# All quarter sums of the part products on VectorE, GpSimd held meanwhile and its state chain one block later, squares on ScalarE, and a new order for the last block and the last products

## The chip, the core and the metric

The kernel runs on one core of one Trainium2 chip. The core has a matrix engine (TensorE, PE in the profile), three engines for elementwise work (VectorE or DVE, ScalarE or ACT, GpSimd or POOL) and SyncE (SP), which here only issues DMAs. Each engine works through its own queue in program order and waits on semaphores for the others. The metric is the device time of one execution in microseconds, the median of the runs shown.

## The reference

Two layers follow each other. The first is a retention layer with 8 batches, 8 heads, 576 positions and 64 columns a head; its result, 4608 rows of 512, is the input x of a feed-forward layer with 2048 hidden columns.

```python
gamma = 1.0 - 2.0 ** (-5.0 - np.arange(H, dtype=np.float32))
Dmat = np.where(rel >= 0, gamma[:, None, None] ** rel[None, :, :], 0.0)
ret = scores * Dmat[None, :, :, :]          # scores = q k^T / sqrt(64)
attn = np.matmul(ret, v)
...
h = x @ w_in
s = np.sin(alpha * h)
g = h + s * s / (alpha + 1e-09)
out = g @ w_out
```

All inputs and the output are float32; the kernel works in float16 with float32 accumulation.

## The kernel before, in words

The 4608 rows are handled as 9 blocks of 512: block b is the first 512 positions of batch b, and block 8 (NBLK is 9, its input is the tile xS) holds the last 64 positions of all batches. The order of instructions on every engine is written out by hand; there is no scheduler. Up to block 2 it is a flat list, from block 3 on the loop `for n in range(3, NBLK)`.

One block of the feed-forward layer is 16 units, one for each 128 hidden columns. A unit u is: `project` (4 matmuls of 512 columns into a bank of PSUM, tile hps, line 550), `sine` on ScalarE (tile s, 558), `square` (tile ss, ScalarE at 567, VectorE or GpSimd at 569) and `product` on VectorE (574), which writes g transposed into gT and frees the bank. Three banks, h0 to h2, are taken in turn, so a projection can start when the product three units before it (two, where attention has taken a bank) is done.

The second matmul, g times w_out, runs one block later, between the projections of the next block. Up to block 2 it is done plainly (`gemm2`, 593, and `finish`). From block 3 on gT and w_out are cut into quarters, and seven products of quarters, M1 to M7, take the place of eight (Strassen's scheme in Winograd's form). `row_sum` (640) makes the sums of gT's quarters S1 to S4, each in two halves p = 0 and 1 (hidden columns 0 to 1023 and 1024 to 2047, that is units 0 to 7 and 8 to 15); S3 is written over a quarter of gT, S1 and S4 need S2. `weight_sum` (630) makes T1 to T4 of w_out once; T1 is written over a quarter of w_out, which the plain products of block 2 still read in block 3. `part_product` (659) runs one product of 16 matmuls of 256 columns; the list `slots` tells after which pair of units each comes. `after_product` (689 to 703) adds up the results: M1 is copied by ScalarE to the tile low (689); M2 is added in M1's bank and copied by ScalarE to an output tile osb (701); M6 gives the tile mid (691), M7 in the same bank gives a new low (693); M4, M5 and M3 are added to these into osb (703). `store` (674, and 670 for block 8) sends osb out, from SyncE's queue but for the very last pieces; in block 8 each output tile takes 4 DMAs.

The attention of batch n+1 runs within block n: `scores` at two units, `masked` on VectorE (385), and at unit `turns` the value products in two halves, with a mark by GpSimd between them (`told`, an empty instruction on GpSimd that waits for the first half and that the second half waits for), the states' part, and `keep` on ScalarE, which writes xT for the next block. At the same unit `outer` makes the products of k and v of batch n+2, ScalarE evicts them (`evict_bank`), and GpSimd turns them into running states: `chain`, which is `to_state` (347) and `more` (354, 355) for four chunks. GpSimd also casts k, v and q of batch n+2 (195 and 122), one each from unit c0 on, and the ends of the batches (179). The loads that bring them go through SyncE's queue into four raw buffers; a load of q takes the place that a cast of k or v in the same block frees. `crossed` are transposing DMAs of the casts, also on SyncE's queue.

What is done around unit u is collected in two lists: `at_unit(u, ...)` runs after the unit's sine, `behind(u, ...)` after its product. In blocks 4 to 8 the squares of the units in ON_V are on VectorE and the others on ScalarE. Block 3 (`plain`) has rules of its own, since the plain products of block 2 run in it.

Before the change, VectorE makes S3 and S2, and GpSimd makes both halves of S1 and S4 behind unit 1 of the next block. After the last block the seven products of block 8 follow in the order M4, M1, M6, M2, M7, M5, M3, with sums on VectorE and GpSimd in between.

## Time and profile before

| | before |
|---|---|
| runs, us | 317.64, 318.65, 322.0 |
| median, us | 318.65 |
| the profiled execution's own time, us | 316.81 |
| its span, first to last instruction, us | 315.1 |
| mean granted TensorE clock in it | 0.993 |

The profile is of one execution. Its page gives busy times by engine, the share of busy time in 40 slices, the DMA queues, the chain of work that ended last and the costliest groups of instructions. A row of the timeline has start, duration, engine, line and operation, out<-in, the shape, and in brackets the idle time of the engine before it and who ended that. A row of a group has the busy time in us, the mean ns of one, and the idle time before them with its releasers. A row of the table by stretches has, for each engine, the busy us and the count of instructions, then the granted TensorE clock, the DMA engines' busy share and GB/s. A row of the waits has the total in us, how often, and the longest. PE is TensorE's matmuls, PEld its weight loads, SPq and ACTq are DMA issues. Instruction starts can overlap the end of the one before by some 0.1 us, since an engine's pipeline takes the next one early.

### The profile page before, as it was taken

What the parts mean: (1) busy time and instruction counts of PE and PEld (TensorE: products, weight loads), DVE (VectorE), ACT (ScalarE), POOL (GpSimd) and SP (SyncE); (2) the same over time, 40 slices, a digit from 0 to 9 for tenths busy, and PEclk for the clock granted to TensorE, in tenths of its full rate; (3) what the DMA queues carried; (4) which work ended last, traced back from release to release, by engine and by line L of the source; (5) the groups of instructions that cost most, each with busy time, mean ns of one, the idle gap of its engine ahead of it and who ended that gap; (6) DMA issues with size and microseconds to landing.
All of it is one profiled execution on the core that took longest, in us unless ns stands there. A gap on an engine that the chain in (4) does not pass through costs nothing.

```text
span 315.1 us, 8517 instructions
## 1 busy us (share of the span) xinstructions
PE 288.3 (91%) x3480; PEld 183.6 (58%) x3480; DVE 247.5 (79%) x333; ACT 195.1 (62%) x321; POOL 188.5 (60%) x173
## 2 busy tenths in 40 slices
PE   5889999999989999997799989898999999989682
PEld 4676445555445544555366666565767676666471
DVE  2578886976269779979996999799889868987861
ACT  1669837987758967775258655856576566654300
POOL 4793688483877865697944897989225501630420
PEclk9999999999999999999799999999999999999999
DMA  8999999997899789896828878964571122102113
GB/s 225 345 215 213 262 302 312 229 249 206 185 230 180 168 181 253 147 189 131 225 61 118 185 185 223 173 144 122 120 115 37 41 45 68 33 2 67 33 35 101
DMA packets 123527, 50.09 MB, mean 159 GB/s; under 512 B 80480, under 2 KB 121440, under 8 KB 123488
## 3 DMA queue, kind: packets, MB, share of 16 engines
q1 hardware_dynamic: 119968, 45.17, 61.4%
q0 software_dynamic: 2688, 4.19, 7.3%
q8 instruction: 27, 0.44, 0.5%
q10 hardware_dynamic: 832, 0.18, 0.4%
q14 instruction: 12, 0.10, 0.1%
HBM read 36.75 MB, written 9.44 MB: 147 GB/s over the span
## 4 chain that ended last, share of the span: by engine, by line
PE 47%; DVE 25%; DMA 13%; ACT 6%; issue 3%; SPq 2%; POOL 2%; POOLq 0%; DVEq 0%; ACTq 0%
PE hps L550 24%; PE ops L659 12%; PE ops L593 7%; DVE gT L574 7%; DVE ss L569 5%; DMA raw<-in_k_dram 4%; DMA raw<-in_v_dram 4%; DVE S L640 4%; DVE gT L640 3%; DMA w_in<-in_moe_w_in_dram 3%; ACT s L558 2%; DVE ret L385 2%; ACT ss L567 2%; DMA qT<-q 1%; PE o L415 1%
## 5 line engine op out<-in xcount | busy, mean ns | idle before, releaser
L558 ACT ACTIVATE s<-hps,alpha_t 128x512 f16<-128x512 f32 x144 | 97.3, 683 | 65.5 <-PE hps L550 64.6
L550 PE MATMUL hps<-xT,w_in 128*128 128x512 f16 (+1 forms) x532 | 123.3, 374 | 5.3 <-DVE gT L574 4.8
L574 DVE SCALAR_TENSOR_TENSOR gT<-ss,inva,hps 128x512 f16<-128x512 f16 x144 | 105.8, 744 | 28.0 <-ACT ss L567 24.1
L550 PEld LDWEIGHTS <-w_in 128*128 128x128 f16 x596 | 66.8, 114 | 59.1 <-issue 10.2
L640 POOL TENSOR_TENSOR S<-gT,S 128x1024 f16<-128x1024 f16 x22 | 49.1, 2252 | 49.8 <-DVE S L640 42.0
L567 ACT ACTIVATE ss<-s 128x512 f16<-128x512 f16 x84 | 52.7, 630 | 2.3
L593 PE MATMUL ops<-w_out,gT 128*128 128x512 f16 x192 | 46.8, 380 | 0.0
L659 PEld LDWEIGHTS <-gT 128*128 128x128 f16 x384 | 36.8, 98 | 10.2 <-DVE gT L574 1.8
L569 DVE TENSOR_TENSOR ss<-s 128x512 f16<-128x512 f16 x52 | 38.1, 735 | 5.2 <-ACT s L558 5.2
L195 POOL TENSOR_TENSOR k<-raw,cn 128x1024 f16<-128x1024 f32 (+1 forms) x17 | 29.4, 1734 | 8.4 <-DMA raw<-in_k_dram 6.9
L659 PEld LDWEIGHTS <-S 128*128 128x128 f16 x288 | 28.0, 98 | 9.2 <-issue 1.6
L593 PEld LDWEIGHTS <-gT 128*128 128x128 f16 x192 | 17.9, 98 | 20.4
L195 POOL TENSOR_TENSOR q<-raw,cn 128x1024 f16<-128x1024 f32 x13 | 25.1, 1938 | 6.4 <-DMA raw<-in_q_dram 4.9
L659 PE MATMUL ops<-T,gT 128*128 128x256 f16 x192 | 23.3, 273 | 2.0 <-DVE gT L574 1.5
L659 PE MATMUL ops<-w_out,S 128*128 128x256 f16 x192 | 23.1, 273 | 1.3 <-DVE osb L703 1.3
L659 PE MATMUL ops<-w_out,gT 128*128 128x256 f16 x192 | 23.0, 273 | 0.0
L385 DVE TENSOR_TENSOR ret<-sc,mask 128x1024 f16<-128x1024 f32 x16 | 19.2, 1220 | 2.9 <-PE sc L373 2.9
L355 POOL TENSOR_TENSOR kvs<-s,kvs 128x256 f32<-128x256 f32 x21 | 17.4, 830 | 3.7 <-ACT kvs L120 1.3
L347 POOL TENSOR_TENSOR s<-kvs,cn 128x256 f16<-128x256 f32 x17 | 10.8, 635 | 11.3 <-PE o L437 7.6
L550 PE MATMUL hps<-xS,w_in 128*128 128x512 f16 x64 | 15.6, 379 | 1.5 <-DVE gT L574 1.4
L354 POOL TENSOR_TENSOR s<-kvs,cn 128x256 f32<-128x256 f32 x21 | 13.0, 620 | 6.5 <-ACT kvs L120 6.4
L373 PE MATMUL sc<-qT,kT 64*64 64x128 f16 (+1 forms) x512 | 11.4, 222 | 4.7 <-DVE ret L385 3.5
(78 smaller groups left out, 286.3 us busy)
## 6 DMA issues: line engine op xcount, KB each, us to landing
raw<-in_q_dram SPq DMA_DIRECT2D x16, 512.0 KB, 4.7
out_dram<-osb SPq DMA_DIRECT2D x64, 128.0 KB, 2.6
raw<-in_k_dram SPq DMA_DIRECT2D x8, 512.0 KB, 6.4
raw<-in_v_dram SPq DMA_DIRECT2D x8, 512.0 KB, 6.5
raw<-in_v_dram SPq DMA_DIRECT2D x32, 128.0 KB, 3.2
raw<-in_k_dram SPq DMA_DIRECT2D x32, 128.0 KB, 3.0
w_in<-in_moe_w_in_dram POOLq DMA_DIRECT2D x4, 512.0 KB, 11.6
w_out<-in_moe_w_out_dram POOLq DMA_DIRECT2D x4, 512.0 KB, 12.9
```

The costliest lines, as they stand in the source:

```text
L195: eng.tensor_tensor(dst[:, a0:a1].rearrange("p a r t d -> p t (a r) d"), t_.rearrange("p (t a) x -> p t a x", t=2)[:, :, a0:a1].rearrange( ...
L354: nc.gpsimd.tensor_tensor(s32, self.kvs[:, c - 1], g1.unsqueeze(2).to_broadcast([P, 4, D]), MULT)
L355: nc.gpsimd.tensor_tensor(self.kvs[:, c], s32, self.kvs[:, c], ADD)
L385: nc.vector.tensor_tensor(ret.rearrange("p t (z x) -> p (t z) x", z=2)[:, :, 0:n], sc.rearrange("p t (z x) -> p (t z) x", z=2)[:, :, 0:n], ...
L550: matmul(hps_of[n, fc][0][:, cols], w_in16[fc // 4][:, a, fc % 4 :: 4], xs[n][:, a, cols], start=(a == 0 and part != 1), stop=(a == KT - 1 ...
L558: nc.scalar.activation(s_t, hps, mybir.ActivationFunctionType.Sin, bias=0.0, scale=alpha_t[:, fc : fc + 1],)
L567: nc.scalar.activation(ss_t, s_t, mybir.ActivationFunctionType.Square)
L569: eng.tensor_tensor(ss_t, s_t, s_t, MULT)
L574: nc.vector.scalar_tensor_tensor(gT[n][:, fc, :], ss_t, inva[:, fc : fc + 1], hps, MULT, ADD)
L593: matmul(ops[n, c, cols.start][:, cols], gT[n][:, fk, c * P : (c + 1) * P], w_out16[:, fk, cols], start=(fk == 0), stop=(fk == FC - 1), sk ...
L640: eng.tensor_tensor(out_, x, y, op)
L659: matmul(acc[:, 256 * j : 256 * j + 256], lhs[:, x, 128 * j : 128 * j + 128], rhs[:, x], start=(tag is not None and j == 0 and p == 0 and ...
```

## The change

1. GpSimd makes no sums any more. VectorE makes all of them: S3, S2, S1 and S4 of the first half behind units 11, 13 and 15 of the block itself, those of the second half behind units 0, 1 and 2 of the next block.
2. Behind unit 2 an empty instruction on GpSimd waits for the last sum, and only then comes the state chain, which stood at unit 13 of the block before. The casts start one unit later (c0 is 5, not 4).
3. In blocks 4 and 5 only the squares of units 12, 13 and 14 are on VectorE, in blocks 6 to 8 those of 2, 6, 10, 12, 13 and 14. The squares of units 1 and 3 go to ScalarE, where they stand behind the copies of M1 and M2.
4. In block 3 the weight sums move from units 5 to 10 to units 0, 1, 2, 10, 11 and 12, and T1 comes from block 4 into its units 14 and 15.
5. In block 8 the units are worked in the order 0 to 7, 12 to 15, 8 to 11. After it the products come in the order M2, M4, M1, M6, M7, M5, M3, with M2, M6 and the two halves of M3 in banks of their own. VectorE adds M2's result and M5's (through mid) instead of adding in PSUM and copying on ScalarE.

```diff
     def part_product(n, i, tag, js=(0, 1), first=None):
...
-            parts[n, i] = psum.tile([P, 512], F32, tag=tag, bufs=1, name="ops")
+            parts[n, i] = bank(tag)
...
-                        start=(tag is not None and j == 0 and p == 0 and x == 0),
+                        start=(tag is not None and j == js[0] and p == 0 and x == 0),
...
-    def after_product(n, i, js=(0, 1), issue=(nc.sync, nc.sync)):
+    def after_product(n, i, js=(0, 1), issue=(nc.sync, nc.sync), apart=False, more=False):
...
-            if i == 2:
+            source = kept["mid" if i == 3 else "low"]
+            if more:
+                nc.vector.tensor_tensor(kept["mid"], acc, kept["mid"], ADD)
+            if i == 2 and not apart:
                 nc.scalar.copy(osb[:, cols], acc[:, cols])
             else:
-                nc.vector.tensor_tensor(osb[:, cols], acc[:, cols], kept["mid" if i == 3 else "low"][:, cols], ADD)
+                nc.vector.tensor_tensor(osb[:, cols], acc[:, cols], source[:, cols], ADD)
...
+            late, turns = (8, 12) if plain else (7, 13)
+            c0 = 3 if plain else 5
+            if not plain:
+                behind(0, lambda: row_sum(n - 1, "S3", 1, V), lambda: row_sum(n - 1, "S2", 1, V))
+                behind(1, lambda: row_sum(n - 1, "S1", 1, V))
+                behind(2, lambda: told(row_sum(n - 1, "S4", 1, V), G_))
+                if n < 7:
+                    behind(2, lambda: at[n + 1].chain((0, 1, 2, 3)))
...
-                    behind(turns, lambda: at[n + 2].chain((0, 1, 2, 3)))
-                behind(turns if not plain else 13, lambda: A.keep(1, A_))
+                behind(13, lambda: A.keep(1, A_))
...
-                c0 = 3 if plain else 4
...
-                for i, (nm, p) in enumerate((("T3", 0), ("T3", 1), ("T2", 0), ("T2", 1), ("T4", 0), ("T4", 1))):
-                    behind(5 + i, lambda nm=nm, p=p: weight_sum(nm, p, V))
-                behind(11, lambda: row_sum(3, "S3", 0, V))
-                behind(14, lambda: row_sum(3, "S2", 0, V))
-            else:
-                if n < 8:
-                    behind(11, lambda: row_sum(n, "S3", 0, V))
-                    behind(15, lambda: row_sum(n, "S2", 0, V))
-                behind(0, lambda: row_sum(n - 1, "S3", 1, V))
-                behind(1, lambda: row_sum(n - 1, "S2", 1, V))
-                for nm in ("S1", "S4"):
-                    for p in range(2):
-                        behind(1, lambda nm=nm, p=p: row_sum(n - 1, nm, p, G_))
-                if n == 4:
-                    behind(2, lambda: weight_sum("T1", 0, V))
-                    behind(4, lambda: weight_sum("T1", 1, V))
+                for u, nm, p in ((0, "T3", 0), (1, "T3", 1), (2, "T2", 0), (10, "T2", 1), (11, "T4", 0), (12, "T4", 1), (14, "T1", 0), (15, "T1", 1)):
+                    behind(u, lambda nm=nm, p=p: weight_sum(nm, p, V))
+            behind(11, lambda: row_sum(n, "S3", 0, V))
+            behind(13, lambda: row_sum(n, "S2", 0, V))
+            behind(15, lambda: row_sum(n, "S1", 0, V), lambda: row_sum(n, "S4", 0, V))
...
-            ON_V = (1, 3, 6, 8, 12, 13) if A else (1, 3, 4, 6, 8, 10, 12, 13)
+            ON_V = (12, 13, 14) if n < 6 else (2, 6, 10, 12, 13, 14)
+            units = [*range(8), *range(12, 16), *range(8, 12)] if n == 8 else [*range(16)]
...
         n = NBLK - 1
+        part_product(n, 2, next(h))
         part_product(n, 4, next(h))
+        row_sum(n, "S3", 1, V)
+        row_sum(n, "S2", 1, V)
         part_product(n, 1, "op")
         after_product(n, 1)
-        for p in range(2):
-            row_sum(n, "S3", p, V)
-            row_sum(n, "S2", p, V)
-        row_sum(n, "S1", 0, G_)
+        part_product(n, 6, "m0")
         row_sum(n, "S1", 1, V)
-        row_sum(n, "S4", 0, G_)
         row_sum(n, "S4", 1, V)
-        part_product(n, 6, next(h))
         after_product(n, 6)
-        part_product(n, 2, None, first=1)
-        after_product(n, 2)
+        after_product(n, 2, apart=True)
         part_product(n, 7, None, first=6)
         after_product(n, 7)
         after_product(n, 4)
         part_product(n, 5, next(h))
-        after_product(n, 5)
-        for j in range(2):
-            part_product(n, 3, None, (j,), first=5)
+        after_product(n, 5, more=True)
+        for j, tag in enumerate(("m1", "op")):
+            part_product(n, 3, tag, (j,))
             after_product(n, 3, (j,), (nc.sync, nc.scalar))
```

More of the change, by code (lines that the diff above doesn't have):

```diff
@@ L1258, in behind @@
                 after.setdefault(u, []).extend(fs)
+            late, turns = (8, 12) if plain else (7, 13)
[6 more added lines that the diff above has]
+                    behind(2, lambda: at[n + 1].chain((0, 1, 2, 3)))
             if A:
-                late = 8 if plain else 7
-                turns = 12 if plain else 13
                 at_unit(3, lambda: A.scores(0, 0, next(m)), lambda: A.scores(0, 1, next(m)))
@@ L1325, with unit_start, unit_end @@
                     behind(9 + i, lambda i=i: E[i // 2].keep(i % 2, A_))
-            def unit_start(u):
+            def unit_start(i, u):
                 project(n, u, next(h))
                 sine(n, u)
-                for f in todo.get(u, []):
+                for f in todo.get(i, []):
                     f()
-            def unit_end(u, eng):
+            def unit_end(i, u, eng):
                 square(n, u, eng)
                 product(n, u)
-                for f in after.get(u, []):
+                for f in after.get(i, []):
                     f()
@@ L1365 @@
                 u = 2 * i
-                unit_start(u)
-                unit_end(u, V if u in ON_V else A_)
-                unit_start(u + 1)
+                unit_start(u, units[u])
+                unit_end(u, units[u], V if u in ON_V else A_)
+                unit_start(u + 1, units[u + 1])
                 if slots[i] is not None:
```

10 lines of the change are left out of this document (5 added, 5 removed).

## The prediction

> **What bounds the kernel now.** First the page: TensorE is busy 91% of the span, so it paces the kernel, and what can be won are its gaps and what hangs on behind its last product.
>
> ```profile
> span 315.1 us, 8517 instructions
> PE 288.3 (91%) x3480; PEld 183.6 (58%) x3480; DVE 247.5 (79%) x333; ACT 195.1 (62%) x321; POOL 188.5 (60%) x173
> ```
>
> Then the table by stretches, cut near the block borders (blocks 4, 5, 6, 8 and the tail). The stretch less PE's busy time is the gap: 4.7, 2.6, 1.1, 1.5 and 10.7 us; block 7 (235 to 263) had 0.15.
>
> ```profile
> 130.00:170.00 40.00, 35.34 (x426) 22.30 (x419) 35.88 (x42) 22.88 (x36) 28.99 (x25) 0.96 0.76 146
> 170.00:203.00 33.00, 30.42 (x395) 20.86 (x394) 29.45 (x35) 22.48 (x36) 28.97 (x24) 1.00 0.86 189
> 203.00:235.00 32.00, 30.92 (x347) 21.67 (x345) 27.79 (x36) 20.90 (x33) 20.33 (x19) 1.00 0.66 133
> 263.00:291.00 28.00, 26.46 (x176) 17.96 (x175) 23.57 (x32) 16.57 (x26) 8.77 (x4) 1.00 0.16 38
> 291.00:316.00 25.00, 14.30 (x117) 10.97 (x115) 13.43 (x16) 3.69 (x6) 4.96 (x2) 0.96 0.21 53
> ```
>
> The waits from 130 us on say who ends the gaps: VectorE, each time, with a product (L574) or a masked score tile (L385).
>
> ```profile
> PE hps L550 <- DVE gT L574: 6.2, 9, 2.3
> PE sc L373 <- DVE ret L385: 3.5, 3, 1.9
> ```
>
> Why VectorE is late is seen in its timeline at the start of block 4. A square takes 0.41 us, or 2.33 us while GpSimd runs three sums from 144.06 to 150.97; a sum takes 0.68 us between GpSimd's sums and 2.61 us across one.
>
> ```profile
> 139.59 2.61 DVE L640 TENSOR_TENSOR gT<-gT 128x1024 f16<-128x1024 f16 x1
> 142.12 0.41 DVE L569 TENSOR_TENSOR ss<-s 128x512 f16<-128x512 f16 x1
> 143.24 0.68 DVE L640 TENSOR_TENSOR S<-gT 128x1024 f16<-128x1024 f16 x1
> 146.66 2.33 DVE L569 TENSOR_TENSOR ss<-s 128x512 f16<-128x512 f16 x1
> 144.06 6.91 POOL L640 TENSOR_TENSOR S<-gT,S 128x1024 f16<-128x1024 f16 x3 [2.41 <-PE ops L659]
> 149.83 1.34 PE L550 MATMUL hps<-xT,w_in 128*128 128x512 f16 x4 [2.33 <-DVE gT L574]
> 155.56 0.37 PE L373 MATMUL sc<-qT,kT 64*64 64x128 f16 x16 [1.88 <-DVE ret L385]
> ```
>
> So the last wait in these stages is: GpSimd's sum delays VectorE's square or sum, that delays the product that frees a projection bank, and PE stands.
>
> **Loads of the engines after.** The groups by line give the prices.
>
> ```profile
> L640 POOL TENSOR_TENSOR S<-gT,S 128x1024 f16<-128x1024 f16 x22 | 49.1, 2252 | 49.8 <-DVE S L640 42.0 <-PE scs L472 4.4 <-PE ops L659 3.4
> L574 DVE SCALAR_TENSOR_TENSOR gT<-ss,inva,hps 128x512 f16<-128x512 f16 x144 | 105.8, 744 | 28.0 <-ACT ss L567 24.1 <-POOL ss L569 2.3
> L558 ACT ACTIVATE s<-hps,alpha_t 128x512 f16<-128x512 f32 x144 | 97.3, 683 | 65.5 <-PE hps L550 64.6 <-DVE ret L385 0.4
> L567 ACT ACTIVATE ss<-s 128x512 f16<-128x512 f16 x84 | 52.7, 630 | 2.3
> L385 DVE TENSOR_TENSOR ret<-sc,mask_halved 128x768 f16<-128x768 f32 x16 | 15.2, 950 | 0.0
> L703 DVE TENSOR_TENSOR osb<-ops,low 128x512 f32<-128x512 f32 x12 | 8.3, 690 | 5.2 <-PE ops L659 5.0
> L120 ACT CAST xT<-o 128x1024 f16<-128x1024 f32 x10 | 10.1, 1024 | 0.2 <-PE o L437 0.2
> L689 ACT COPY low<-ops 128x512 f32<-128x512 f32 x6 | 3.5, 587 | 7.6 <-PE ops L659 7.6
> ```
>
> All 22 sums of GpSimd (49.1 us) go to VectorE. At the undisturbed 0.68 us that adds 15 us there, while 10 squares leave it. A block with attention then costs VectorE 16 products x 0.744 + 8 sums x 0.68 + 3 squares x 0.41 + 4 masks x 0.95 + 5 evictions x 0.69 = 25.8 us, and ScalarE 16 sines x 0.683 + 13 squares x 0.63 + 2 evictions of x at 1.02 + 4 copies at 0.587 = 23.5 us. PE needs 30.4 us (its busy time in 170 to 203). Neither becomes the bound by its sum; what counts is lateness at the block border.
>
> **The border of block 4, step by step.** Two rows of the chain price PE's steps: a projection 0.86 us, a part product 1.75 us; block 4's first projection starts at 136.34.
>
> ```profile
> 107.37 0.86 PE hps L550 x4
> 163.41 1.75 PE ops L659 x16
> 136.34 1.89 PE L550 MATMUL hps<-xT,w_in 128*128 128x512 f16 x8
> 137.69 0.75 DVE L574 SCALAR_TENSOR_TENSOR gT<-ss,inva,hps 128x512 f16<-128x512 f16 x1 [0.95 <-ACT ss L567]
> ```
>
> VectorE's new queue: product 15 of block 3 at 137.7 (it waits for ScalarE, as now), T1's second half, S1 and S4 of the first half (to 140.5), product 0 (141.1), S3 and S2 (142.5), product 1 (143.2), S1, product 2 (144.5), S4 (145.2), product 3 (145.9), mask (146.8). PE: projections 0 and 1 to 138.1, product M1 to 139.8, projection 2 to 140.7; projection 3 needs product 0's bank and waits 0.5; then scores, M2, projections 4 and 5, M6 end at 147.9 with no wait, because products 1 and 2 (143.2, 144.5) come before their banks are asked for (144.4, 145.3). Projection 6 starts at 147.9 in place of 149.83. The matmuls after the present 2.33 us gap also run slow (1.34 us for 4, granted clock 0.96 in this stretch), which goes too. The second pair of scores then starts at about 150.2, not 155.56: 5.4 us won. I give back 0.5 later in the block (casts, below): **4.9**. Square 1 now stands on ScalarE behind the copy of M1 (139.8 + 0.59 + 0.63 = 141.0): covered by VectorE's queue, which reaches product 1 only at 142.5. Without that cover it would cost at most the 0.9 us by which it comes later than now.
>
> **Block 5.** Product 12 is late because a sum and a square meet GpSimd's last casts; PE stands 1.16 us.
>
> ```profile
> 197.59 1.43 DVE L640 TENSOR_TENSOR gT<-gT 128x1024 f16<-128x1024 f16 x1
> 198.95 1.26 DVE L569 TENSOR_TENSOR ss<-s 128x512 f16<-128x512 f16 x1
> 201.04 1.02 PE L550 MATMUL hps<-xT,w_in 128*128 128x512 f16 x4 [1.16 <-DVE gT L574]
> 186.49 1.90 POOL L195 TENSOR_TENSOR k<-raw,cn 128x1024 f16<-128x1024 f32 x1
> 194.32 1.90 POOL L195 TENSOR_TENSOR q<-raw,cn 128x1024 f16<-128x1024 f32 x1 [1.92 <-DMA raw<-in_q_dram]
> 198.44 1.49 POOL L179 TENSOR_TENSOR ks<-ks,cn 128x512 f16<-128x512 f32 x1
> 201.07 0.79 POOL L347 TENSOR_TENSOR s<-kvs,cn 128x256 f16<-128x256 f32 x1
> 207.78 0.61 POOL L347 TENSOR_TENSOR sS<-kvs,cn 128x256 f16<-128x256 f32 x1
> ```
>
> The hold adds a wait: GpSimd stands until the last sum S4, about 7.6 us after block 5's first projection by the same walk (8.9 in block 4, where T1 stands ahead). Queued behind it are the state chain (201.07 to 208.4: 7 us), six casts, and the marks that the second half of the value products waits for. The chain ends at +14.6, where the first cast starts; now it starts at 186.49, some 14.3 us after block 5's first projection, since 9 us of sums stand ahead of it. So the casts keep their place. The q loads keep the slots that the first casts free (load to cast, 188.39 to 194.32, as now), and the marks come near +26, where PE asks at +25.5. I leave a wait of 0.5 there, and 1.2 for the collision above: of 2.6 us, **0.9** is won. Block 6 has only the chain: of 1.1, **0.7**. Block 8 has no GpSimd work left at all: **1.4**.
>
> One rule speaks against the change. The Trainium skill (SBUF — State Buffer, Who interferes with whom) says that a VectorE instruction with two SBUF inputs and a GpSimd one that reads SBUF exclude each other, the later one waiting for the whole of the earlier. By it the first-half sums and the three squares left at positions 11 to 15 would each wait out a cast; the rows 197.59 and 198.95 agree in kind (0.75 and 0.85 us more). What that gives is the second rival.
>
> **Block 3** loses: T3 and half of T2 move to positions 0 to 2, beside casts of k, and PE has no gap there to lend. One sum behind a 1.9 us cast makes product 2 about 0.8 late: **-0.8** (bounds 0 and -2).
>
> **The tail.** Now PE ends its last projection at 291.07. The order written there waits for the last units, then runs sums on both engines, and stores begin at 302.92; 14 stores at 0.6 us each end at 312.6, the span 2.5 later.
>
> ```profile
> 290.19 0.88 PE hps L550 x4
> 302.92 9.66 SPq L670 DMA_DIRECT2D out_dram<-osb  x14
> 306.15 2.38 SPq L670 DMA_DIRECT2D out_dram<-osb  x4
> 312.04 0.54 SPq L670 DMA_DIRECT2D out_dram<-osb  x1
> ```
>
> After: from the end of the last projection (T), M2 and M4 need only units 0 to 7 and 12 to 15, which are done; they cover the last products and S3, S2 (done near T+5.4). M1, M6 end at T+7.2; mid 0.69, then the first output tile at T+8.6. From there SyncE issues its 14 stores without a break, 8.6 us, and 2.5 us remain: T+19.7, against 315.1 - 291.07 = 24.0. **4.3**. Low bound: SyncE keeps its present 9.66, so 3.2. High bound: stores never queue, last output tile at T+13.7 plus 0.6 and 2.5, so 7.2.
>
> **Sum.** 4.9 + 0.9 + 0.7 + 1.4 - 0.8 + 4.3 = 11.4 us. The profiled execution took 316.81 us beside a span of 315.1, which gives 305.4. The three runs (317.64, 318.65, 322.0) lie above the profiled one; I put the forecast a little up: **306.0 us**. All gaps gone, clock too and the tail's high bound would be 18 us: 299. With block 3 at -2 and the marks 2 us late in blocks 4 and 5: 311.
>
> **Rivals.**
> *GpSimd becomes the wait.* If the load of q lags or S4 comes 3 us later, the marks are late in blocks 4 and 5 by 2 to 3 us each, and scores in the next block by less. Against it: nothing of GpSimd's 9 us of sums is left, so it can only be late by the hold. Gain 6 us, 311. Chance 0.10.
> *The collision follows the work.* Sums at 11, 13, 15 and squares at 12 to 14 meet casts in blocks 3, 4, 5. Six instructions, each late by up to 0.85 (row 198.95) make 5 us in a block; VectorE's slack of 30.4 - 25.8 = 4.6 lies earlier in the block and does not help. Some 3 us lost in each of three blocks: gain 2 to 3, so 314 to 316. For it: that is just where blocks 4 to 5 stand now. Against: in block 4 the same sum met no cast and took 0.68. Chance 0.10.
> *The sums are slow by themselves.* Then 8 x 2.25 in place of 8 x 0.68 brings VectorE to 38.4 us a block, 8 over PE, in five blocks: +40 less the tail, about 352. It decides from 1.3 us a sum (no gain) and 1.5 (over 2% slower). For it: the mean of 2252 and VectorE's own long ones. Against: every VectorE sum outside GpSimd's spans took 0.68. Chance 0.05, on the slower side.
>
> **How the numbers follow.** Forecast 0.75, its own range 301 to 311; rivals 0.10, 0.10, 0.05. Two per cent of 318.65 is 6.4 us, about what a measurement tells from no change: faster is below 312.3, slower above 325. Faster gets 0.75 less 0.02 for a forecast that falls short, and 0.08 of the first rival: 0.81; same 0.02 + 0.02 + 0.10 = 0.14; slower 0.05. The range runs from 300.5 to 314.5.
>
> **What would show it.** Right: VectorE's sums near 0.7 us at the borders, no PE gap over 1 us in blocks 4 and 6, granted clock 1.00 from 130 to 170, the first store some 9 us after the last projection, SyncE busy without a break. Wrong: PE waiting on value products for GpSimd's marks, sums above 1.3 us with GpSimd idle, or ScalarE's queue ending PE's waits.

## The result and the profile after

| us | before | after |
|---|---|---|
| median of the runs shown together | 320.32 (317.64 to 322.09, 4 runs) | 307.69 (306.89 to 309.57, 4 runs) |
| the profiled execution's own time | 316.81 | 308.11 |
| its span | 315.1 | 306.4 |

After takes 0.9621 of the time before, with a 95% interval of 0.9525 to 0.9717. The forecast was 306.0 with a range of 300.5 to 314.5.

The page of the changed kernel, first line and busy times. The span is 8.7 us shorter. TensorE runs the same 3480 matmuls, but is busy 4.2 us less (288.3 to 284.1); its time without work fell by 4.5 us (26.8 to 22.3). So only about half of the difference is lost gaps; the other half is matmuls that take less time, a third of it in block 4 (below). VectorE has 14 instructions more (22 sums and 2 additions of the last products came, 10 squares went), yet is busy 13.6 us less, and GpSimd 52.5 us less.

```profile
span 306.4 us, 8511 instructions
PE 284.1 (93%) x3480; PEld 182.7 (60%) x3480; DVE 233.9 (76%) x347; ACT 199.0 (65%) x330; POOL 136.0 (44%) x151
```

Why VectorE is busy less with more to do is in the groups by line (count, then busy us and mean ns). The 24 sums S1 and S4 take 0.684 us each there, where GpSimd needed 2.252; the other sums fell from 1163 and 1050 ns to 837 and 693.

```profile
L640 DVE TENSOR_TENSOR S<-gT,S 128x1024 f16<-128x1024 f16 x24 | 15.8, 684 | 0.0
L640 DVE TENSOR_TENSOR gT<-gT 128x1024 f16<-128x1024 f16 x12 | 10.0, 837 | 0.0
L640 DVE TENSOR_TENSOR S<-gT 128x1024 f16<-128x1024 f16 x12 | 8.3, 693 | 0.2
```

The waits from 125 us on (total, times, longest): PE's waits for VectorE's products fell from 6.2 to 3.9 us and those for masked scores from 3.5 to 0.8. GpSimd's hold shows as three waits of some 12 us of the state chain, and it costs nobody anything: no wait of PE for a mark is among them.

```profile
POOL s L347 <- DVE S L640: 35.7, 3, 13.1
PE hps L550 <- DVE gT L574: 3.9, 7, 1.4
PE sc L373 <- DVE ret L385: 0.8, 3, 0.3
```

The border of block 4 in the timeline of the changed kernel, from its first projections to the second scores, which come 13.7 us later (13.9 in the prediction). T1's halves take 0.69 and 0.68, the sums 0.64 to 0.68, and GpSimd stands until 146.88.

```profile
138.19 0.69 DVE L630 TENSOR_TENSOR w_out<-w_out 128x1024 f16<-128x1024 f16 x1
138.34 1.89 PE L550 MATMUL hps<-xT,w_in 128*128 128x512 f16 x8
140.35 0.68 DVE L630 TENSOR_TENSOR w_out<-w_out 128x1024 f16<-128x1024 f16 x1
140.95 1.28 DVE L640 TENSOR_TENSOR S<-gT,S 128x1024 f16<-128x1024 f16 x2
142.81 0.68 DVE L640 TENSOR_TENSOR gT<-gT 128x1024 f16<-128x1024 f16 x1
146.88 0.61 POOL L347 TENSOR_TENSOR s<-kvs,cn 128x256 f16<-128x256 f32 x1 [13.12 <-DVE S L640]
152.07 0.37 PE L373 MATMUL sc<-qT,kT 64*64 64x128 f16 x16 [0.28 <-DVE ret L385]
```

From the rows of each block's first projections (as the row at 138.34; before it stood at 136.34, 172.23, 204.83, 234.89, 263.81) and of the last pair of block 8 (290.02 before, 284.04 after) the length of each block can be taken. The tail runs from that last pair to the end of the span. The same rows of the experiments, which follow, are in the table too.

| us | start of block 4 | block 4 | 5 | 6 | 7 | 8 | tail |
|---|---|---|---|---|---|---|---|
| before | 136.34 | 35.89 | 32.60 | 30.06 | 28.92 | 26.21 | 25.08 |
| **after** | 138.34 | **30.58** | **31.49** | **29.09** | **29.37** | **25.17** | **22.36** |
| after, its second profile | 144.15 | 30.51 | 31.57 | 29.09 | 29.39 | 25.16 | 22.33 |
| f1, weight sums alone | 139.41 | 32.42 | 32.00 | 30.06 | 28.90 | 26.21 | 25.10 |
| f2, squares alone | 140.46 | 34.01 | 31.69 | 30.04 | 30.46 | 24.56 | 24.78 |
| e4, sums alone | 137.57 | 33.53 | 34.17 | 29.79 | 29.83 | 25.57 | 23.04 |
| e5, last block and tail alone | 136.48 | 37.95 | 32.88 | 30.06 | 28.91 | 26.23 | 22.39 |
| e1, after with GpSimd's sums | 137.57 | 31.55 | 33.66 | 29.10 | 30.47 | 25.16 | 22.39 |
| e2, after without the hold | 140.13 | 32.90 | 33.36 | 29.09 | 29.37 | 25.16 | 22.39 |
| e3, after with the old squares | 138.99 | 31.16 | 32.12 | 29.09 | 28.88 | 24.70 | 22.36 |
| e6, stores on two queues | 137.86 | 30.53 | 32.06 | 29.09 | 29.37 | 25.16 | 20.43 |
| e7, square 12 on ScalarE | 140.39 | 30.06 | 30.10 | 29.09 | 29.38 | 25.17 | 22.41 |
| e8, combined | 136.77 | 29.98 | 30.13 | 29.09 | 28.81 | 24.70 | 20.42 |
| e9, M5 on GpSimd's queue | 140.43 | 30.03 | 30.94 | 29.09 | 28.82 | 24.70 | 21.09 |

How far to trust it: each row is one profile. The two profiles of the changed kernel differ by 5.8 us at the start of block 4, in a first part that no experiment was aimed at, and by at most 0.08 in every block after it. But e6, which has the changed kernel's instructions up to the tail, is 0.57 longer in block 5, and e5, which has those of the kernel before up to block 7, is 2.06 longer in block 4. So differences of some 0.6 us in block 5 decide nothing, and in block 4 the length has to be taken apart. The second profile of the changed kernel (313.98 us) and that of e9 (306.84 us) are of slow executions, over 1.5% above the fastest run of the same kernel, and no experiment but e9 is read from them alone.

Cut at the same rows, the table by stretches gives PE's busy time in block 4. The rest is gap. The matmuls are the same in all rows; what their busy time varies by goes mostly with the granted clock.

| block 4, us | length | PE busy | gap | granted clock |
|---|---|---|---|---|
| before | 35.89 | 31.23 | 4.66 | 0.95 |
| e5, the same instructions | 37.95 | 33.42 | 4.53 | 0.87 |
| **after** | **30.58** | **29.75** | **0.83** | **1.00** |
| f1, weight sums alone | 32.42 | 30.30 | 2.12 | 1.00 |
| f2, squares alone | 34.01 | 31.09 | 2.92 | 0.95 |
| e4, sums alone | 33.53 | 29.71 | 3.82 | 1.00 |

So 3.8 of the 5.3 us that block 4 won are gap, and 1.5 are faster matmuls. e5's 2.06 are all clock; its gap is that of before within 0.13.

From before to after the blocks and the tail give 5.31 + 1.11 + 0.97 - 0.45 + 1.04 + 2.72 = 10.7 us. Block 3 gives 0.86 of it back: counted 16 projections back from the start of block 4, it starts at 105.48 before and at 106.62 after, and takes 30.86 and 31.72 us. The two profiled executions differ by 8.7, since block 4 of this profile of after starts 2.0 later: 0.86 from block 3, and 1.1 from ahead of it, where the instructions are the same.

### The profile page after: what moved, and what is told of

It reads as the page before. It is cut to its first block, busy times and chain, and to the rows that moved or that the text cites. A ratio compares the mean times of both kernels' runs of the same rounds, so it can differ in the third digit from the quotient of the medians.

```text
span 306.4 us, 8511 instructions
## 1 busy us (share of the span) xinstructions
PE 284.1 (93%) x3480; PEld 182.7 (60%) x3480; DVE 233.9 (76%) x347; ACT 199.0 (65%) x330; POOL 136.0 (44%) x151
## 4 chain that ended last, share of the span: by engine, by line
PE 65%; DMA 12%; DVE 12%; ACT 3%; issue 2%; SPq 2%; POOL 1%; POOLq 0%; DVEq 0%; ACTq 0%
PE hps L550 30%; PE hps L659 23%; PE ops L593 7%; DVE gT L574 4%; DMA raw<-in_v_dram 3%; DMA w_in<-in_moe_w_in_dram 3%; DMA raw<-in_k_dram 3%; DVE ss L569 2%; PE sc L373 2%; DMA qT<-q 2%; DVE gT L640 1%; DVE ret L385 1%; PE o L415 1%; POOL k L195 1%; SPq L586 1%
## 5 line engine op out<-in xcount | busy, mean ns | idle before, releaser
L550 PE MATMUL hps<-xT,w_in 128*128 128x512 f16 (+1 forms) x532 | 121.6, 371 | 4.1 <-DVE gT L574 3.1
L567 ACT ACTIVATE ss<-s 128x512 f16<-128x512 f16 x94 | 59.0, 630 | 2.3
L195 POOL TENSOR_TENSOR k<-raw,cn 128x1024 f16<-128x1024 f32 (+1 forms) x17 | 29.0, 1706 | 11.4 <-DMA raw<-in_k_dram 11.4
L659 PEld LDWEIGHTS <-S 128*128 128x128 f16 x288 | 28.1, 98 | 6.0
L569 DVE TENSOR_TENSOR ss<-s 128x512 f16<-128x512 f16 x42 | 22.0, 527 | 5.2 <-ACT s L558 5.1
L659 PE MATMUL hps<-T,gT 128*128 128x256 f16 x192 | 23.0, 273 | 0.9 <-DVE mid L691 0.9
L659 PE MATMUL hps<-w_out,gT 128*128 128x256 f16 x192 | 23.0, 273 | 0.2 <-DVE gT L574 0.2
L659 PE MATMUL hps<-w_out,S 128*128 128x256 f16 x192 | 22.8, 273 | 0.0
L355 POOL TENSOR_TENSOR kvs<-s,kvs 128x256 f32<-128x256 f32 x21 | 16.1, 768 | 4.1 <-ACT kvs L120 1.4
L640 DVE TENSOR_TENSOR S<-gT,S 128x1024 f16<-128x1024 f16 x24 | 15.8, 684 | 0.0
L385 DVE TENSOR_TENSOR ret<-sc,mask_halved 128x768 f16<-128x768 f32 x16 | 15.2, 948 | 0.0
```

Source lines behind the costliest of these rows:

```text
L195: eng.tensor_tensor(dst[:, a0:a1].rearrange("p a r t d -> p t (a r) d"), t_.rearrange("p (t a) x -> p t a x", t=2)[:, :, a0:a1].rearrange( ...
L355: nc.gpsimd.tensor_tensor(self.kvs[:, c], s32, self.kvs[:, c], ADD)
L385: nc.vector.tensor_tensor(ret.rearrange("p t (z x) -> p (t z) x", z=2)[:, :, 0:n], sc.rearrange("p t (z x) -> p (t z) x", z=2)[:, :, 0:n], ...
L550: matmul(hps_of[n, fc][0][:, cols], w_in16[fc // 4][:, a, fc % 4 :: 4], xs[n][:, a, cols], start=(a == 0 and part != 1), stop=(a == KT - 1 ...
L567: nc.scalar.activation(ss_t, s_t, mybir.ActivationFunctionType.Square)
L569: eng.tensor_tensor(ss_t, s_t, s_t, MULT)
```

## The experiments

### e1: GpSimd's work as it was before

```diff
...
-                behind(1, lambda: row_sum(n - 1, "S1", 1, V))
-                behind(2, lambda: told(row_sum(n - 1, "S4", 1, V), G_))
-                    behind(2, lambda: at[n + 1].chain((0, 1, 2, 3)))
+                for nm in ("S1", "S4"):
+                    for p in range(2):
+                        behind(1, lambda nm=nm, p=p: row_sum(n - 1, nm, p, G_))
...
+                    behind(turns, lambda: at[n + 2].chain((0, 1, 2, 3)))
...
```

> The changed kernel with GpSimd's part as it was in blocks 4 to 8: it makes the four halves of S1 and S4 behind unit 1, the chain stands at unit 13 of the block before, no hold, casts from unit 4. Squares, weight sums, last block and tail stay changed. Theory (collision: GpSimd's sums hold up VectorE's squares and sums at the block borders): blocks 4 to 6 lose most of what they won, 5 us of 7.4, block 8 about 1; 6 us slower than the changed kernel, near 314. Rival (the squares: VectorE was simply overloaded, and ten squares fewer and later ones made the gain): within 1.5 us of the changed kernel.

Measured: 312.09 us (308.43 to 313.76, 4 runs), 0.9688 of before (0.9572 to 0.9804); 4.4 above the changed kernel by median. The direction is the theory's (some 6 slower), but block 4 is only 1.0 longer, not most of the gain, and block 8, where about 1 was expected, is unchanged. The timeline of e1 shows why: GpSimd's sums now meet a single two-input instruction of VectorE there, S3. T1 has been done ahead of them, and squares 1 and 3 are on ScalarE.

```profile
142.13 2.12 POOL L640 TENSOR_TENSOR S<-gT,S 128x1024 f16<-128x1024 f16 x1
142.28 2.53 DVE L640 TENSOR_TENSOR gT<-gT 128x1024 f16<-128x1024 f16 x1
146.21 4.22 POOL L640 TENSOR_TENSOR S<-gT,S 128x1024 f16<-128x1024 f16 x2 [1.95 <-PE hps L659]
```

In block 7 the square of unit 2, which the changed kernel has on VectorE, meets them, and block 7 is 1.1 longer:

```profile
238.94 6.48 POOL L640 TENSOR_TENSOR S<-gT,S 128x1024 f16<-128x1024 f16 x3 [5.88 <-DVE S L640]
239.85 1.50 DVE L569 TENSOR_TENSOR ss<-s 128x512 f16<-128x512 f16 x1
242.19 1.02 PE L550 MATMUL hps<-xT,w_in 128*128 128x512 f16 x4 [1.59 <-DVE gT L574]
```

Block 5 is 2.2 longer, but GpSimd's sums make no wait there. PE's gap is 0.55 longer, since the cast of q meets S3 and the square of unit 12 at the end of the block (PE waits 1.95 at 197.32, 1.40 in the changed kernel; e6, whose sums are on VectorE, has 1.98 at that place), and the other 1.6 are matmuls at a granted clock of 0.95.

So it is not a property of the sums where they run; what costs is a pair, a two-input instruction of VectorE beside a GpSimd instruction on SBUF. With GpSimd's sums left in place, but T1 and the squares out of their way, block 4 is still 4.3 of the 5.3 us shorter than before.

### e2: the changed kernel without the hold

```diff
-                behind(2, lambda: told(row_sum(n - 1, "S4", 1, V), G_))
+                behind(2, lambda: row_sum(n - 1, "S4", 1, V))
```

> The changed kernel without the empty instruction that holds GpSimd until the last sum; the chain may start as soon as its inputs are there. Theory (collision): the chain's seven two-input steps now run beside the border sums, which go from 0.68 to about 1.0 to 1.3 us each; VectorE is 2 us later at three borders, PE has at most 1 us of room there, and the casts come 7 us earlier, which takes away the 1.4 us wait in block 5; in sum 0 to 3 us slower. Rival (the hold only delays GpSimd): sums stay at 0.68 and the kernel is 1 to 2 us faster.

Measured: 312.86 us (311.6 to 315.97, 4 runs), 0.9776 of before (0.9692 to 0.986). The blocks say +2.3 in block 4 and +1.9 in block 5, more than the theory's 0 to 3 for all; the rival (the hold costs) is out. The wait at the end of block 5, which was to go, is still 1.11: the casts of q wait for their loads and come only 0.5 to 0.6 us earlier in the block. GpSimd, held by nothing, runs ahead of VectorE through the chain and into the first cast of k, and meets the sums:

```profile
143.02 1.07 POOL L347 TENSOR_TENSOR sS<-kvs,cn 128x256 f16<-128x256 f32 x1
143.54 3.41 DVE L640 TENSOR_TENSOR S<-gT,S 128x1024 f16<-128x1024 f16 x2
144.05 2.35 POOL L195 TENSOR_TENSOR k<-raw,cn 128x1024 f16<-128x1024 f32 x1
147.66 1.02 PE L550 MATMUL hps<-xT,w_in 128*128 128x512 f16 x4 [2.42 <-DVE gT L574]
```

### e3: the changed kernel with the old squares

```diff
-            ON_V = (12, 13, 14) if n < 6 else (2, 6, 10, 12, 13, 14)
+            ON_V = (1, 3, 6, 8, 12, 13) if A else (1, 3, 4, 6, 8, 10, 12, 13)
```

> The changed kernel with the squares of blocks 4 to 8 shared out as before (six or eight a block on VectorE). Theory (collision): VectorE has 25.8 + 1.2 us a block, still under PE, and the squares at units 1 and 3 leave ScalarE's copies; 0 to 1.5 us slower, no more. Rival (the squares made the gain): 4 us or more slower.

Measured: 308.56 us (306.67 to 311.66, 4 runs), 0.9608 of before (0.9532 to 0.9684), as the theory had it. With GpSimd held, squares 1 and 3 cost VectorE 0.42 each at the border, and no wait of PE follows from them. The blocks show that the new places cut both ways: they win 0.6 in block 4 (0.6 in block 5 too, about what two profiles of the same instructions differ by there) and lose 0.5 in blocks 7 and 8 each.

### e4: the kernel before with its 22 sums on VectorE, and nothing else

```diff
-                        behind(1, lambda nm=nm, p=p: row_sum(n - 1, nm, p, G_))
+                        behind(1, lambda nm=nm, p=p: row_sum(n - 1, nm, p, V))
...
-        row_sum(n, "S1", 0, G_)
+        row_sum(n, "S1", 0, V)
-        row_sum(n, "S4", 0, G_)
+        row_sum(n, "S4", 0, V)
```

> The kernel before with one edit: the 22 sums of GpSimd go to VectorE at their places, nothing else is changed; GpSimd runs its casts beside them. Theory (collision): GpSimd's 49 us of sums are gone, but its casts now start at the border and hit the same sums, four of them in a row behind unit 1; half of the gain, 3 to 6 us faster than before. Rival (sums are dear on VectorE, or VectorE is the bound): no faster than before, or slower.

Measured: 316.16 us (315.21 to 318.4, 4 runs), 0.9875 of before (0.9805 to 0.9945), so 4.4 faster by median. Block 4 wins 2.4 and block 5 loses 1.6. In both, four sums in a row behind unit 1 hold the product of unit 2, and a cast of k, which no longer has 9 us of GpSimd's own sums ahead of it, meets a sum of VectorE. The rows are those of block 4:

```profile
140.76 1.90 POOL L195 TENSOR_TENSOR k<-raw,cn 128x1024 f16<-128x1024 f32 x1
140.82 2.39 DVE L640 TENSOR_TENSOR gT<-gT 128x1024 f16<-128x1024 f16 x1
145.69 2.49 DVE L640 TENSOR_TENSOR S<-gT,S 128x1024 f16<-128x1024 f16 x4
148.89 1.02 PE L550 MATMUL hps<-xT,w_in 128*128 128x512 f16 x4 [2.64 <-DVE gT L574]
```

Most of the two numbers is clock. In block 4 the gap fell by only 0.8 and PE's busy time by 1.5. In block 5 the gap is 2.68 against 2.58 before; PE waits 2.40 there (at 182.19), the granted clock is 0.83 from 180 to 190, and the busy time is 1.5 longer.

### f1: the kernel before with only the weight sums moved

```diff
-                for i, (nm, p) in enumerate((("T3", 0), ("T3", 1), ("T2", 0), ("T2", 1), ("T4", 0), ("T4", 1))):
-                    behind(5 + i, lambda nm=nm, p=p: weight_sum(nm, p, V))
+                for u, nm, p in ((0, "T3", 0), (1, "T3", 1), (2, "T2", 0), (10, "T2", 1), (11, "T4", 0), (12, "T4", 1), (14, "T1", 0), (15, "T1", 1)):
+                    behind(u, lambda nm=nm, p=p: weight_sum(nm, p, V))
...
-                if n == 4:
-                    behind(2, lambda: weight_sum("T1", 0, V))
-                    behind(4, lambda: weight_sum("T1", 1, V))
```

> The kernel before with only the weight sums moved: T3 and T2 to units 0, 1, 2, 10 of block 3, T4 to 11, 12, T1 out of block 4 into units 14, 15 of block 3. GpSimd keeps its sums, the squares stay on VectorE. Theory A (block 4's 5.3 us are those of pairs of T1, S3, S2 and squares with GpSimd's sums, and T1's two halves at 2.2 us each were the largest of them): block 4 shorter by 2.5 to 4 us, P0 of block 4 later by 0 to 1.5, the time 2 to 3.5 below before. Theory B (whatever two-input work stands there waits, and products are late by GpSimd's 9 us in any case): block 4 shorter by under 1 us, the time within 1 of before.

Measured: 314.45 us (313.01 to 315.78, 4 runs), 0.9866 of before (0.9821 to 0.9911). Block 4 is 3.5 shorter (2.5 of it gap), as theory A expected; theory B falls. The time is 5.4 below before by median, more than the 2 to 3.5 expected; blocks 4 and 5 give 4.1. The start of block 4 is 3.1 later, but 2.6 of that lie in block 2, which the edit does not touch, and 0.4 in block 3. T1's halves take 1.13 and 0.87 beside short instructions of GpSimd. GpSimd's three sums still run for 6.46 us, but only one square meets them, and the wait of PE behind it is 0.50.

```profile
139.96 1.13 DVE L630 TENSOR_TENSOR w_out<-w_out 128x1024 f16<-128x1024 f16 x1
142.69 0.87 DVE L630 TENSOR_TENSOR w_out<-w_out 128x1024 f16<-128x1024 f16 x1
148.52 6.46 POOL L640 TENSOR_TENSOR S<-gT,S 128x1024 f16<-128x1024 f16 x3 [2.42 <-DVE S L640]
148.95 1.97 DVE L569 TENSOR_TENSOR ss<-s 128x512 f16<-128x512 f16 x1
153.28 1.02 PE L550 MATMUL hps<-xT,w_in 128*128 128x512 f16 x4 [0.50 <-DVE gT L574]
```

### f2: the kernel before with only the squares moved

The diff is that of e3 turned round.

> The kernel before with only the squares moved: those of VectorE at units 12, 13, 14 in blocks 4 and 5, at 2, 6, 10, 12, 13, 14 from block 6 on. GpSimd keeps its sums, T1 stays in block 4. Theory A (T1 and the squares of units 1 and 3 each waited out a sum of GpSimd, T1 with the larger share): block 4 shorter by 1 to 2.5, block 5 longer by 0 to 1 since three squares stand beside its casts, the time 1 to 3 below before. Theory B (one of the two is enough, since products are late only where both meet): block 4 shorter by 3 or more.

Measured: 316.91 us (314.65 to 319.2, 4 runs), 0.9873 of before (0.9782 to 0.9963). Block 4 is 1.9 shorter, 1.7 of it gap, at before's granted clock: theory A. The time is 4.3 below before by median, more than the 1 to 3 expected, in an interval that reaches from 1 to 7. T1 is still in the way of GpSimd's sums, and its second half ends in the longest wait of PE for VectorE that any profile shows from block 4 on.

```profile
147.08 6.76 POOL L640 TENSOR_TENSOR S<-gT,S 128x1024 f16<-128x1024 f16 x3 [0.69 <-DVE S L640]
147.52 2.25 DVE L630 TENSOR_TENSOR w_out<-w_out 128x1024 f16<-128x1024 f16 x1
151.87 2.51 DVE L630 TENSOR_TENSOR w_out<-w_out 128x1024 f16<-128x1024 f16 x1
156.56 0.37 PE L373 MATMUL sc<-qT,kT 64*64 64x128 f16 x16 [2.92 <-DVE ret L385]
```

Its expectation for block 5 (0 to 1 longer) missed: it is 0.9 shorter. Block 7 is 1.5 longer; square 2 stands on VectorE there, beside GpSimd's sums, as in e1. Block 8 is 1.65 shorter. Alone, the three parts win 3.5 (weight sums), 1.9 (squares) and 2.4 (sums) in block 4, 7.7 in all, together 5.3: they do not add up. Of the gap they win 2.5, 1.7 and 0.8, and together 3.8, since they share one cause; of the busy time 0.9, 0.1 and 1.5, and together 1.5, since the lost clock can be won back only once.

### e5: the kernel before with only the last block's order and the last products

```diff
-                unit_start(u)
+                unit_start(u, units[u])
...
         n = NBLK - 1
+        part_product(n, 2, next(h))
         part_product(n, 4, next(h))
...
```

> The kernel before with only the last block's part of the change: its units in the order 0 to 7, 12 to 15, 8 to 11, its first-half sums behind units 13 and 15, and the new order of the last products. Everything up to block 7 is as before. Theory (the tail's gain is the products that need only done units, and it is bounded by the 14 stores): from the start of the last pair of projections to the end 22.4 us as in the changed kernel, against 25.1, and block 8 shorter by 0 to 1; the time 2.5 to 4 us below before. Rival (the tail gains only because VectorE and ScalarE come to it less late, from the other parts): less than 1 us below before.

Measured: 316.61 us (315.63 to 317.91, 8 runs), 0.9912 of before (0.9875 to 0.9948): 3.2 faster by median. The tail is 22.39 as in the changed kernel (22.36), so its 2.7 need no other part; block 8 is unchanged, so after's 1.0 there comes from elsewhere (in f2 the squares alone win 1.65 there). The tail's last stores run without a break:

```profile
303.14 9.25 SPq L670 DMA_DIRECT2D out_dram<-osb  x14
```

### e6: the changed kernel with the last stores on two queues

```diff
-        after_product(n, 2, apart=True)
+        after_product(n, 2, issue=(nc.sync, nc.scalar), apart=True)
...
-        after_product(n, 4)
+        after_product(n, 4, issue=(nc.sync, nc.scalar))
-        after_product(n, 5, more=True)
+        after_product(n, 5, issue=(nc.sync, nc.scalar), more=True)
```

> The changed kernel with the stores of M2's, M4's and M5's tiles shared half and half between SyncE's and ScalarE's queues. Theory (SyncE's issue of 14 stores in a row, 9.2 us, sets the end from the first store on): the end then hangs on the last product M3 and its two stores, 17 to 18 us after the last projection in place of 20.6, so 2.5 to 3.5 us below the changed kernel. Rival (the transfers themselves or M3 set the end): within 1 us of the changed kernel.

Measured: 306.32 us (305.81 to 307.12, 4 runs), 0.9614 of before (0.9583 to 0.9644). The tail is 1.9 shorter (20.43), between the theory's 2.5 to 3.5 and the rival's 1. The run times do not show it for themselves: 0.9614 of before, against 0.9621 for the changed kernel. Each queue issues 8 stores, from 294.7 to 301.5 and 301.8 with a break, since M4's and M5's tiles come one after the other; the last product's tile is done at 300.0. So the issue was the bound, and in part still is.

```profile
294.70 6.82 SPq L670 DMA_DIRECT2D out_dram<-osb  x8
294.71 7.12 ACTq L670 DMA_DIRECT2D out_dram<-osb  x8
299.03 0.96 DVE L706 TENSOR_TENSOR osb<-hps,mid 128x256 f32<-128x256 f32 x2
```

### e7: the changed kernel with square 12 on ScalarE

```diff
-            ON_V = (12, 13, 14) if n < 6 else (2, 6, 10, 12, 13, 14)
+            ON_V = (13, 14) if n < 6 else (2, 6, 10, 12, 13, 14)
```

> The changed kernel with the square of unit 12 on ScalarE in blocks 4 and 5. Theory (in block 5 the square of unit 12 takes 2.12 us beside the cast of q and makes PE wait 1.40): that wait falls below 0.5, block 5 is shorter by 0.8 to 1.4, the time by about 1. Rival (the next two-input instruction, S2 or the square of unit 13, takes its place beside the cast): the wait moves by one or two units and block 5 stays within 0.4.

Measured: 308.83 us (305.65 to 309.38, 4 runs), 0.9669 of before (0.9593 to 0.9745). By median that is no gain, but its profile starts block 4 2.0 later than after's; block 5 is 1.39 shorter, and the wait is gone, as the theory said; the projection behind it waits 0.21 (0.16 in the changed kernel). The rival is not quite out, though: which instruction the cast of q meets depends on when q's load has landed. In e6, with the same instructions as the changed kernel, it is S3 (2.32) and then the square (1.26), and PE waits 1.98. The timeline of the changed kernel there, then that of e7:

```profile
193.37 2.12 POOL L195 TENSOR_TENSOR q<-raw,cn 128x1024 f16<-128x1024 f32 x1 [0.18 <-DMA raw<-in_q_dram]
193.66 2.12 DVE L569 TENSOR_TENSOR ss<-s 128x512 f16<-128x512 f16 x1
196.62 1.02 PE L550 MATMUL hps<-xT,w_in 128*128 128x512 f16 x4 [1.40 <-DVE gT L574]
```

```profile
196.68 1.06 PE L550 MATMUL hps<-xT,w_in 128*128 128x512 f16 x4
197.94 1.02 PE L550 MATMUL hps<-xT,w_in 128*128 128x512 f16 x4 [0.21 <-DVE gT L574]
```

### e8: the fixes together, and e9: a third queue

```diff
 e8, beside e6:
-            ON_V = (12, 13, 14) if n < 6 else (2, 6, 10, 12, 13, 14)
+            ON_V = (13, 14) if n < 6 else (2, 6, 10, 12, 13, 14) if n != 7 else (6, 10, 12, 13)
-                for u, nm, p in ((0, "T3", 0), (1, "T3", 1), (2, "T2", 0), (10, "T2", 1), (11, "T4", 0), (12, "T4", 1), (14, "T1", 0), (15, "T1", 1)):
+                for i, (nm, p) in enumerate((("T3", 0), ("T3", 1), ("T2", 0), ("T2", 1), ("T4", 0), ("T4", 1))):
+                    behind(5 + i, lambda nm=nm, p=p: weight_sum(nm, p, V))
+                for u, nm, p in ((14, "T1", 0), (15, "T1", 1)):
 e9, beside e8:
-        after_product(n, 5, issue=(nc.sync, nc.scalar), more=True)
+        after_product(n, 5, issue=(nc.gpsimd, nc.gpsimd), more=True)
```

> The changed kernel with four edits: the last stores shared between SyncE's and ScalarE's queues, the square of unit 12 on ScalarE in blocks 4 and 5, the squares of units 2 and 14 on ScalarE in block 7, and T3, T2, T4 of block 3 back at units 5 to 10 (T1 stays at 14 and 15). Theory (each of the waits left has one late instruction of VectorE as its cause, and the edits take it away): the wait of 1.40 in block 5 falls to 0.2, those of 0.50 in block 7 and 0.66 at the start of block 8 vanish, that of 0.65 in block 3 too, and the tail is 1.9 shorter: about 4.5 to 5 in all, 302.5 to 304. Rival (the waits move to the next instruction): only the tail's 1.9 is left, 305.5 to 306.5.

> As e8_combined, and the four stores of M5's tile issued from GpSimd's queue, which is empty by then. Theory (the two queues still issue without a break from M4's tile on, so the last store comes 1.2 after M3's last result): the tail is another 1.0 to 1.3 shorter. Rival (an issue from GpSimd takes longer and lands later, and ends the span): no gain, up to 2 longer.

> The changed kernel once more, beside the combined ones on one chip: 307 to 309, the same waits as in its first profile.

Measured on one chip: e8 303.59 us (301.6 to 306.13, 4 runs), 0.9437 of before (0.9338 to 0.9535); e9 304.61 (302.23 to 306.84, 4 runs), 0.9465 (0.9364 to 0.9565); the changed kernel again 308.64 (307.83 to 313.98, 4 runs), 0.9606 (0.952 to 0.9693). By its blocks e8 is 0.60 + 1.36 + 0.00 + 0.56 + 0.47 + 1.94 = 4.9 us shorter than the changed kernel, as its theory expected (4.5 to 5), and it is the fastest version by median. The waits at the starts of blocks 7 and 8 are gone or down to 0.20. In block 3 the rival was right: with T3, T2 and T4 back at units 5 to 10 it takes 31.98 us, not less than the changed kernel's 31.72; in place of the wait of 0.65 there are one of 0.71 and one of 0.35, a little earlier. The profiled execution, the shortest of the four, was also lucky ahead of the change: its block 2 takes 24.68 us, 1.7 less than in the profile of after.

```profile
256.04 1.02 PE L550 MATMUL hps<-xS,w_in 128*128 128x512 f16 x4 [0.20 <-DVE gT L574]
```

The changed kernel once more came out as expected (307 to 309), with the same waits of PE from 125 us on within 0.2 in their sums.

e9 follows its rival: the tail is 0.7 longer than e8's; the run times of the two do not differ clearly. Its stores on the other two queues end at 300.5 and 300.8, but GpSimd's four end at 301.5 and the span 3.6 us after that; in e8 it ends 2.65 after the last issue (290.12 + 7.13 = 297.25, span 299.9).

```profile
294.64 5.87 SPq L670 DMA_DIRECT2D out_dram<-osb  x6
294.64 6.15 ACTq L670 DMA_DIRECT2D out_dram<-osb  x6
299.34 2.16 POOL L670 DMA_DIRECT2D out_dram<-osb  x4 [70.97 <-DVE osb L706]
```

The Trainium skill (DMA: Bandwidth & Descriptors, Specifications) gives a first-byte latency of about 1 us for a DMA issued from GpSimd against 0.6 from SyncE or ScalarE; the trace agrees in kind, with 1.0 us more here.

## Why the prediction was right, and where it was off

**What bounds it, and block 4.** Right. The walk along VectorE's queue put the second scores 13.9 us after the block's start, measured 13.7; the gain was put at 4.9, measured 5.31. Half a microsecond had been given back for casts and marks, and no wait for a mark came. That the matmuls behind the gap ran slow, and that this goes too, was named but not priced; it is 1.5 of the 5.3, and it differs from run to run (e5). What the prediction did not separate is which of VectorE's instructions GpSimd's sums hit: it quoted sums and squares, but T1, which it only carried along in the queue, is the largest part (f1: 3.5 of 5.3). The parts overlap, so the sum was right without the split.

**The hold.** Right in place and price: the chain was to start 8.9 us after block 4's start and 7.6 after block 5's, and began at 8.5 and 7.6. That the hold would be needed for the gain was only implied; e2 prices it at 4.2 us in two blocks.

**Block 5** was put at 0.9 and won 1.1 (0.5 in e6, with the same instructions), but the rival "the collision follows the work" is true in one place: square 12 beside the cast of q, 1.40 of waiting. The 1.2 that the prediction left for it was about what e7 gave back. The rule of the Trainium skill named there (SBUF — State Buffer, Who interferes with whom: the later instruction waits for the whole of the earlier) fits: the cast ends at 193.37 + 2.12 = 195.49, the square at 195.78. Priced by it at six places, that rival had been too large: in block 5 one of the six was hit in full in this profile, and in e6, with the same instructions, another one in full and the next in part (2.32 and 1.26). The other two rivals are out: nobody waits for GpSimd's marks, and a sum with GpSimd idle takes 0.68.

**Blocks 6, 7 and 8.** 0.7, 0 and 1.4 in the sum, 0.97, -0.45 and 1.04 measured. The step that failed is the treatment of the new squares as free from block 6 on. In block 7 the square of unit 2 stands behind a sum and a mask of 1.22, and the product behind it makes PE wait 0.50; the square of unit 14 and S2 ahead of it make block 8's second projection wait 0.66. Without them (e3, e8) the blocks take 28.9 or 28.8 and 24.7. The timeline of the changed kernel in block 7:

```profile
236.34 1.22 DVE L481 TENSOR_TENSOR rets<-scs,mask 128x1024 f16<-128x1024 f32 x1
237.47 0.41 DVE L569 TENSOR_TENSOR ss<-s 128x512 f16<-128x512 f16 x1
238.72 1.02 PE L550 MATMUL hps<-xT,w_in 128*128 128x512 f16 x4 [0.50 <-DVE gT L574]
```

**Block 3** was put at -0.8, and the two profiles give -0.86. The size came out by luck, for it is another wait: 0.65 (at 134.88), behind T4's first half of 1.33 and S3 of 1.53 beside GpSimd's casts of the ends. At the place that the prediction walked through, the first half of T2 does meet a cast of k (1.69 in place of 0.68), but PE waits for nothing there. Over all profiles the changed kernel's block 3 takes 31.7 to 32.7 us, the old one 30.9 in three profiles and 32.0 in f2.

**The tail** is the term that was mis-sized: 4.3 against 2.72, below its own low bound of 3.2. Two things were wrong in it. First, the end of the last projection was taken as 291.07 from a row of the chain (290.19 0.88) that holds only half of the last pair; the timeline of the kernel before has the pair at 290.02, and at 1.73 us for 8 matmuls it ends at 291.75, so the old tail was 0.7 shorter than said. Second, 14 stores take 9.24 us, not 8.6, and the first comes at 8.9, not 8.6, after the last projection. The pair in the kernel before:

```profile
290.02 1.89 PE L550 MATMUL hps<-xS,w_in 128*128 128x512 f16 x8
```

The same pair and the stores in the changed kernel:

```profile
284.04 1.89 PE L550 MATMUL hps<-xS,w_in 128*128 128x512 f16 x8
294.67 9.24 SPq L670 DMA_DIRECT2D out_dram<-osb  x14
```

The mechanism held: SyncE issues without a break, and e6 shows that this is what ends the kernel. The low bound had been built on the present 9.66, and so contained the second error, but not the first.

**The sum.** 11.4 us had been predicted, and the same terms measured give 10.7 - 0.86 = 9.8; the difference of 1.6 is the tail's, and the other terms, each off by less than 0.5, cancel out. The two medians differ by 12.6, the two profiled executions by 8.7; the forecast of 306.0 had been made against the profiled one and lies 1.7 under the median measured. That it lies so near is in part luck: it was set beside one execution, and the runs of one kernel range over 2.7 us (after) and 4.5 us (before).

## What to carry to other kernels

Look for pairs, not for a slow engine: where a two-input VectorE instruction and a GpSimd instruction on SBUF meet ahead of a product that frees PE's bank, moving one of them away can win much of the time (here 1.9 to 3.5 of 5.3 us in block 4), and an empty waiting instruction on GpSimd is a cheap way to keep the pair apart. Several edits that remove the same pair must not be added up. Take a block's length apart into gap and busy time before you compare two profiles: the same gaps came with 2.2 us more of busy time in e5. In a tail, count the DMA issues of the last engine and their price each, and take both ends of the stretch from rows that show the whole of the last work.

## What the runs showed of the hardware that was not expected

Short gaps of PE cost more than their length. e5 has the same instructions as the kernel before up to block 7 and the same waits in block 4 (2.34 and 1.88; before 2.33 and 1.88), but its block 4 is 2.1 us longer: the granted clock (third number from the end) was 0.55 for 10 us behind them, and 0.91 in the kernel before. After has 1.00 there. The tables by stretches of before, then of e5:

```profile
152.00:162.00 10.00, 8.12 (x79) 5.34 (x78) 9.32 (x11) 3.32 (x5) 9.09 (x6) 0.91 0.58 159
```

```profile
152.00:162.00 10.00, 8.12 (x61) 4.36 (x60) 7.51 (x9) 2.00 (x3) 9.22 (x6) 0.55 0.61 159
156.18 3.59 PE L659 MATMUL hps<-T,gT 128*128 128x256 f16 x16
```

The last row, from the timeline of e5, shows a part product at that clock: 3.59 us where 1.91 is usual. So part of block 4's gain is clock, and it differs from run to run.

In these rows the one that comes second pays in a collision. The cast of k that began 0.5 us after VectorE's sums took 2.35 (row 144.05 of e2); the one that began 0.06 ahead of a sum took 1.90, and the sum 2.39 (rows 140.76 and 140.82 of e4).

Of the 5.8 us by which the start of block 4 differs between the two profiles of the changed kernel, 3.6 come ahead of block 1 and 2.3 in block 2, whose instructions are the same in all runs. Block 2 takes 24.7 to 26.8 us at a granted clock of 1.00 in eight profiles, and 28.1 to 28.6 at 0.94 in the other six. What decides between the two was not studied.
